# A fused recurrent-attention and SOLU kernel: two constants by transfer, the first two weight pieces fetched as one, and a weight conversion put behind the masking

## The chip, the cores and the metric

The kernel runs on one core of one Trainium2 chip. The metric is the device time of that core in microseconds: the median of the runs, lower is better.

## The reference

Four batches, eight heads, 768 tokens, head size 48; then a feed-forward block over the 3072 tokens with a hidden size of 1024. What matters of it:

```python
for t in range(S):
    state = alpha[:, :, t, :, None] * state + einsum('bhd,bhe->bhde', k[:, :, t], v[:, :, t])
    y[:, :, t] = einsum('bhd,bhde->bhe', q[:, :, t], state)
x = y.transpose(0, 2, 1, 3).reshape(B * S, H * D)       # 3072 x 384
h = x @ w_in                                            # 3072 x 1024
solu = h * softmax(h)
ln = (solu - mean(solu)) / sqrt(var(solu) + 1e-6) * g_ln
out = ln @ w_out                                        # 3072 x 384
```

q, k, v, alpha and g_ln are float32. The two weight matrices come in as 64-bit floats, since they are scaled by a 64-bit number when they are made.

## The kernel before

The 768 tokens are cut into six chunks of 128 tokens (`g`, 0 to 5), and each chunk holds all four batches. A chunk first goes through the attention part and then through the feed-forward part. All instructions are written out in one order by hand (a manual schedule), so each engine works through its own queue in the order of the code. From the second chunk on, the attention work of the next chunk is spread by a table of steps over the eight blocks of the up-projection of the present one. The first chunk has its own opening, and this opening is where the change lies.

The opening runs as follows. SyncE issues transfers of the first chunk's alpha, k, q and v (`load_first`, L153, and `load_v_first`, L189) and then of the first weights (`fetch`, L569). ScalarE's queue issues two small ones, `parity` and `g_rows`. GpSimd makes the identity matrix `ident` and the triangular `mask` out of `ones` with two selects (L652), and then fills several tiles with constants. TensorE turns alpha, k and q (`turned`, L171, a product with `ident`), and VectorE runs scans over the turned decay factors (L222) and multiplies keys and queries by them (L694, L704).

Then come the scores of the first chunk. `scores(0, 0)` makes those of heads 0 to 3, `scores(0, 1)` those of heads 4 to 7 (L281). They have to be multiplied by the triangular mask on their way out of PSUM. For heads 0 to 3, batches 2 and 3 are copied by ScalarE (L715) and multiplied by GpSimd (L716); batches 0 and 1 are done by VectorE in `masked(0, range(2))` (L292). Heads 4 to 7 of all four batches are VectorE's, in `masked(1)` (L292 too, out of the tiles a_h and a_o). `read_values(0)` (L315) multiplies the masked scores by the values, batch by batch, each batch needing all its heads; ScalarE copies the results into `x` (L351). `keys_back` (L300) and its copies `kg` (L302) and `next_state` (L364) make the state.

The 64-bit weights arrive as raw words in a tile `room` of six slots (1536 numbers each, per partition). There are eight pieces: pieces 0 to 3 are two blocks each of w_in, pieces 4 to 7 two blocks each of w_out. `fetch(i, slot, n)` transfers `n` pieces, one transfer for each of three (w_in) or two (w_out) row groups. With n = 1 a piece lies flat in its slot; with n = 2 the rows of two pieces lie beside each other over two slots, and each piece is a cut of 256 out of rows of 512 (`raws`). `bits(i)` makes 32-bit floats out of a piece with five VectorE instructions: L599 and L602 (`top`), L607 and L610 (`low`), and L611, which adds the two into the weight tile. `bits(i, 0)` is the first two of them, `bits(i, 1)` the last three. `in_range(i)` checks a piece's range with ScalarE (L586, L587).

The loop `for f in range(FC)` then runs the first chunk's eight up blocks: `up_mm` (L389) on TensorE, and `up_act`, an exponential (ScalarE, L403), a product with the block (VectorE, L404) and a square (ScalarE, L405). Pieces 2 and on are converted between them. Block 0 needs piece 0, block 2 needs piece 1. Behind block 0, `fetch(4, 3)` reuses slot 3, and the second chunk's k, q and alpha are loaded. The products of the first blocks are written into slots of `room` too.

Of the kernel before, what the change touches and what calls it, by code (L numbers as in the profile page):

```python
# [14 lines left out]
ALU = mybir.AluOpType  # L15
AX = mybir.AxisListType
P = 128
# [15 lines left out]
def fast_path(ctx, tc, q, k, v, alpha, moe_w_in, moe_w_out, moe_g_ln, out):  # L33
# [12 lines left out]
    nc = tc.nc  # L46
# [31 lines left out]
    ident = const.tile([P, P], FP, name="ident")  # L78
    mask = const.tile([P, P], FP, name="mask")
    ones = const.tile([P, P], FP, name="ones")  # L80
# [69 lines left out]
    def load_first(src, dst, g):  # L150
        t = slice(g * P, (g + 1) * P)
        for b in range(0, B, 2):
            nc.sync.dma_start(  # L153
                out=by_token(dst)[:, b : b + 2].rearrange("p b h d -> p (b h) d"),
                in_=src[b : b + 2, :, t].rearrange("b h p d -> p (b h) d"),
            )
# [27 lines left out]
    def load_v_first(slot):  # L184
        x = slots[slot].rearrange("p (n d) -> p n d", d=D)
        y = vn.rearrange("p b h d -> p (b h) d")
        xi, yi = (z.rearrange("p (n i) d -> p i n d", i=2) for z in (x, y))
        for b in range(0, B, 2):
            nc.sync.dma_start(  # L189
                out=x[:, H * b : H * b + 2 * H], in_=v[b : b + 2, :, 0:P].rearrange("b h p d -> p (b h) d")  # L190
            )
        for i in range(2):
            nc.gpsimd.tensor_copy(out=yi[:, i, :, all_of[i]], in_=xi[:, i])
# [95 lines left out]
    def masked(half, batches=range(B)):  # L289
        a = masks[half]  # L290
        for b in batches:
            nc.vector.tensor_tensor(  # L292
                out=sT[:, b, half * NP : half * NP + NP], in0=a[b], in1=mask[:, None, :].to_broadcast([P, NP, P]),
                op=ALU.mult,
            )
# [47 lines left out]
    def read_values(g, batches=range(B)):  # L343
        if 0 in batches:
            gr[g]["x"] = pair.tile([P, KC, B, P], FP, name="x")
        for b in batches:
            for n, part in enumerate(parts):
                for a, r, h, e in part:
                    y_mm(b, a, r, 0, vn[:, b, h, e], sT[:, b, h], n == len(parts) - 1)
        for b in batches:  # L350
            nc.scalar.copy(out=gr[g]["x"][:, :, b], in_=reading["y"][b])  # L351
# [200 lines left out]
    def place(i):  # L552
        kind, f = pieces[i]
        return w_out[:, f : f + 2, 0:DM] if kind else w_in[:, :, f * P : f * P + 2 * P]
# [3 lines left out]
    def fetch(i, slot, n=1):  # L558

        kind, f = pieces[i]  # L560
        w = n * F // (2 if kind else KC)
        raw = room[:, 1536 * slot : 1536 * (slot + n)].bitcast(U32).rearrange("p (c f w) -> p c f w", f=w, w=2)
        if kind:
            parts = [(slice(0, P), c, moe_w_out[(f + c) * P : (f + c + 1) * P, :]) for c in range(2)]
        else:
            parts = [(slice(0, P), c, moe_w_in[c * P : (c + 1) * P, f * P : f * P + w]) for c in range(KC)]
        for rows, c, src in parts:
            if float64:
                nc.sync.dma_start(out=raw[rows, c].rearrange("p f w -> p (f w)"), in_=src.bitcast(U32))  # L569
            else:  # L570
                dst = w_out[rows, f + c, 0:DM] if kind else w_in[rows, c, f * P : f * P + w]
                nc.sync.dma_start(out=dst, in_=src)
        for m in range(n):
            raws[i + m] = raw[:, :, w // n * m : w // n * (m + 1)]
# [14 lines left out]
    def bits(i, part=None):  # L589
        if not float64:  # L590
            return
        lo, hi = raws[i][:, :, :, 0], raws[i][:, :, :, 1]
        if part != 1:
            made[i] = [
                two.tile([P, F], FP, tag="two", name=x).rearrange("p (c f) -> p c f", c=hi.shape[1])
                for x in ("top", "low")
            ]
            top = made[i][0].bitcast(U32)
            nc.vector.tensor_scalar(  # L599
                out=top, in0=hi, scalar1=3, scalar2=0x3FFFFFF8, op0=ALU.logical_shift_left, op1=ALU.bitwise_and  # L600
            )
            nc.vector.scalar_tensor_tensor(  # L602
                out=top, in0=hi, scalar=0xC0000000, in1=top, op0=ALU.bitwise_and, op1=ALU.bitwise_or
            )
        if part != 0:
            top, low = made.pop(i)
            nc.vector.tensor_scalar(  # L607
                out=low.bitcast(U32), in0=top.bitcast(U32), scalar1=0xFF800000, scalar2=None, op0=ALU.bitwise_and
            )
            nc.vector.scalar_tensor_tensor(out=low, in0=lo, scalar=2.0**-52, in1=low, op0=ALU.mult, op1=ALU.mult)  # L610
            nc.vector.tensor_tensor(out=place(i), in0=low, in1=top, op=ALU.add)  # L611
# [34 lines left out]
    def inline(x, name):  # L646
        return nc.inline_tensor(np.ascontiguousarray(x, np.float32), name=name).ap()

    load_first(alpha, an, 0)
    nc.vector.memset(ones, 1.0)  # L650
    for x, op in ((ident, ALU.is_equal), (mask, ALU.is_ge)):
        nc.gpsimd.affine_select(  # L652
            out=x, in_=ones, pattern=[[1, P]], compare_op=op, fill=0.0, base=0, channel_multiplier=-1
        )
    odd = np.arange(P) // E1 % 2
    nc.scalar.dma_start(out=parity, in_=inline(np.stack([1 - odd, odd], 1), "parity_c"))
    nc.scalar.dma_start(out=g_rows, in_=moe_g_ln.rearrange("(c p) -> c p", p=P))
# [7 lines left out]
    nc.gpsimd.memset(seed, 0.0)  # L665
    nc.gpsimd.memset(state, 0.0)
    load_v_first(0)
    fetch(0, 3)
    fetch(1, 4)
    fetch(2, 1, 2)  # L670
    nc.vector.memset(small_ones, 1.0 / 32)
    nc.vector.memset(mhalf, -0.5)
    nc.vector.memset(mone, -1.0)
# [26 lines left out]
    for i in (2, 0, 1):  # L700
        if i == 1:
# [3 lines left out]
            out=qe if i == 2 else qv[:, part], in0=t[i], in1=aT[:, part, 1:SW], op=ALU.mult  # L705
# [9 lines left out]
        nc.scalar.copy(out=s, in_=masks[0][b])  # L715
        nc.gpsimd.tensor_tensor(out=s, in0=s, in1=mask[:, None, :].to_broadcast([P, NP, P]), op=ALU.mult)  # L716
    masked(0, range(2))
    bits(0, 0)
    masked(1)
    bits(0, 1)  # L720
    read_values(0)
    gains()
    keys_back(0)
# [225 lines left out]
    def compare(out, x, bound, op):  # L949
# [6 lines left out]
        out=chunks[:, :, 2], in0=sums[:, :, 2], scalar=0.25, in1=sums[:, :, 3], op0=ALU.mult, op1=ALU.is_le  # L956
# [6 lines left out]
    else:  # L963
# [9 lines left out]
        out=bad, in0=all_ok[0:1, 0:1], scalar1=float(P * ends[-1]), scalar2=None, op0=ALU.is_lt  # L973
# [415 lines left out]
def kernel(tc, *args):  # L1389

    with ExitStack() as ctx:
        taken = fast_path(ctx, tc, *args)
    with tc.If(taken > 0):
        general_path(tc, *args)
# [30 lines left out]
```

## Time and profile before

| | |
|---|---|
| median of 3 runs | 382.29 us (382.2 to 382.33) |
| profiled execution, its own time | 382.33 us |
| its span, from the first to the last instruction | 380.6 us |
| granted TensorE clock | 0.998 |
| TensorE busy | 366.1 us, 96% of the span |
| VectorE, ScalarE, GpSimd busy | 244.7, 146.5 and 131.0 us |
| HBM read and written | 25.17 and 4.72 MB |

The rows of the profile give start and length in microseconds, the engine (PE is TensorE, PEld its weight loads, DVE VectorE, ACT ScalarE, POOL GpSimd, SP SyncE), the line of the kernel, the operation, the tile written and the tiles read, shapes as partitions x elements, and a count where several instructions are merged. In square brackets stands how long the engine was idle before and what released it. `room<-h,sT` reads: room is written, from h and sT. Times count from the span's start.

### The profile page before, as it was taken

The page shows a single profiled execution, that of the slowest core. Times are in us where ns is not written, and L with a number is a line of the kernel's source. Part 1 is how long each engine was busy: PE and PEld are TensorE (multiplying, and loading weights), DVE is VectorE, ACT ScalarE, POOL GpSimd, SP SyncE. Part 2 cuts the span into 40 slices and gives each one's busy share as a digit, 9 for nine tenths or more (in the row PEclk, how much of TensorE's full clock was granted, in tenths as well). Part 3 has the DMA queues.
Part 4 walks back from the last instruction along what each step waited for, and adds up shares of the span by engine and source line. Part 5 has one row for each costly group of instructions (what it writes and reads, how often), then busy time and mean ns, then how long its engine had stood idle before and what let it go on. Part 6 is the DMA issues. An engine that isn't in the chain of part 4 may idle for free.

```text
span 380.6 us, 10529 instructions
## 1 busy us (share of the span) xinstructions
PE 366.1 (96%) x4659; PEld 220.3 (58%) x4659; DVE 244.7 (64%) x379; ACT 146.5 (38%) x263; POOL 131.0 (34%) x136
## 2 busy tenths in 40 slices
PE   8869999999998999999999999999999999999995
PEld 8666345557654566555576555575555675555552
DVE  0997878997998776883665874665875411455410
ACT  2627775484355253215351224351224131233110
POOL 5050000041148980663630662630672520333210
PEclk9999999999999999999999999999999999999999
DMA  9994969304089000960001950002400000000011
GB/s 178 182 307 124 213 223 189 88 0 127 24 188 161 7 7 9 199 146 22 22 14 35 208 122 22 23 24 40 67 0 22 22 24 2 22 21 21 22 46 47
DMA packets 65670, 30.65 MB, mean 81 GB/s; under 512 B 47048, under 2 KB 63440, under 8 KB 65616
## 3 DMA queue, kind: packets, MB, share of 16 engines
q1 hardware_dynamic: 64880, 29.11, 34.9%
q8 instruction: 38, 0.62, 0.7%
q10 hardware_dynamic: 736, 0.79, 0.6%
q14 instruction: 16, 0.13, 0.1%
HBM read 25.17 MB, written 4.72 MB: 79 GB/s over the span
## 4 chain that ended last, share of the span: by engine, by line
PE 72%; DVE 15%; ACT 7%; issue 3%; DMA 1%; SPq 0%; ACTq 0%; DVEq 0%
PE o L500 30%; PE h L389 24%; PE y L315 8%; PE a L281 5%; DVE hT L222 3%; DVE room L404 2%; PE warm L445 2%; DVE sT L292 2%; DVE top L602 2%; DMA an<-in_alpha_dram 1%; ACT sq L586 1%; DVE aT L197 1%; PE kv L364 1%; PE tp L300 1%; DVE top L599 1%
## 5 line engine op out<-in xcount | busy, mean ns | idle before, releaser
L500 PE MATMUL o<-w_out,room 128*128 128x385 f32 x384 | 133.8, 491 | 0.0
L389 PE MATMUL h<-x,w_in 128*128 128x512 f32 x288 | 132.3, 598 | 0.5 <-DVE room L404 0.5
L500 PEld LDWEIGHTS o<-w_out,room 128*128 128x128 f32 x384 | 71.2, 190 | 55.8 <-issue 13.7
L389 PEld LDWEIGHTS h<-x,w_in 128*128 128x128 f32 x288 | 52.8, 189 | 59.4 <-issue 48.2
L404 DVE TENSOR_TENSOR room<-h,e 128x512 f32<-128x512 f32 x40 | 27.6, 689 | 81.5 <-ACT e L403 81.4
L403 ACT ACTIVATE e<-h 128x512 f32<-128x512 f32 x40 | 23.9, 596 | 107.6 <-PE h L389 107.6
L420 POOL TENSOR_TENSOR p<-p,e 128x512 f32<-128x512 f32 x30 | 41.8, 1394 | 15.7 <-ACT e L403 15.6
L537 POOL TENSOR_TENSOR r<-sums,mhalf 128x1 f32<-128x1 f32 x20 | 14.9, 746 | 80.6 <-DVE sums L528 80.5
L405 ACT ACTIVATE u<-room 128x512 f32<-128x512 f32 x40 | 25.2, 630 | 38.5 <-DVE room L404 38.5
L292 DVE TENSOR_TENSOR sT<-a,mask 128x512 f32<-128x512 f32 x42 | 26.1, 682 | 8.3 <-PE a L281 8.2
L263 POOL TENSOR_TENSOR state<-state,hT 128x192 f32<-128x192 f32 x20 | 11.2, 580 | 53.7 <-DVE hT L222 53.7
L243 POOL TENSOR_TENSOR kT<-kT,hT 128x1024 f32<-128x1024 f32 (+1 forms) x8 | 14.2, 1798 | 42.6 <-DVE kT L197 34.3
L222 DVE TENSOR_TENSOR_SCAN hT<-aT,unit 128x516 f32<-128x516 f32 x18 | 23.2, 1364 | 8.6 <-ACT aT L686 8.5
L315 PE MATMUL y<-sT,vn 128*32 128x128 f32 x768 | 23.3, 274 | 4.0 <-DVE sT L292 2.9
L281 PEld LDWEIGHTS a<-qv,kT 32*128 32x128 f32 x704 | 21.8, 186 | 9.1 <-issue 2.4
L420 DVE TENSOR_TENSOR p<-p,u 128x512 f32<-128x512 f32 x30 | 22.7, 756 | 6.5 <-ACT u L405 6.5
L222 DVE TENSOR_TENSOR_SCAN aT<-aT,seed 128x516 f32<-128x516 f32 x18 | 26.6, 1510 | 0.2
L281 PE MATMUL a<-qv,kT 32*128 32x128 f32 x704 | 24.5, 278 | 2.3 <-DVE qv L704 0.9
L315 PEld LDWEIGHTS y<-sT,vn 128*32 128x32 f32 x768 | 20.7, 110 | 6.0 <-DVE sT L292 3.1
L214 ACT ACTIVATE sq<-an,mone 128x1536 uint8<-128x1536 f32 x12 | 18.9, 1572 | 0.2
L315 PE MATMUL y<-qv,state 32*32 32x128 f32 x960 | 16.8, 277 | 0.3 <-issue 0.3
L539 ACT ACTIVATE o_sb<-o,r 128x384 f32<-128x384 f32 x16 | 9.3, 580 | 18.8 <-POOL r L537 18.8
(148 smaller groups left out, 376.3 us busy)
## 6 DMA issues: line engine op xcount, KB each, us to landing
an<-in_alpha_dram SPq DMA_DIRECT2D x20, 192.0 KB, 4.0
vn<-in_v_dram SPq DMA_DIRECT2D x10, 384.0 KB, 6.2
out_dram<-o_sb SPq DMA_DIRECT2D x20, 192.0 KB, 1.9
room<-in_moe_w_out_dram SPq DMA_DIRECT2D x8, 384.0 KB, 3.6
kn<-in_k_dram SPq DMA_DIRECT2D x16, 192.0 KB, 4.7
qn<-in_q_dram SPq DMA_DIRECT2D x16, 192.0 KB, 3.5
kn<-in_k_dram SPq DMA_DIRECT2D x4, 384.0 KB, 5.6
qn<-in_q_dram SPq DMA_DIRECT2D x4, 384.0 KB, 5.7
```

The costliest lines, as they stand in the source:

```text
L214: nc.scalar.activation(out=sq, in_=x, func=AF.Relu, scale=sign, bias=mone, accum_out=over[:, g, i : i + 1])
L222: nc.vector.tensor_tensor_scan(out=o, data0=a, data1=s, initial=1.0, op0=ALU.mult, op1=ALU.add)
L281: nc.tensor.matmul(a[b][:, i], lhsT=kT[quarter(b), kb], rhs=qv[quarter(b), qb], start=kb == h, stop=kb != h, tile_position=(32 * b, 0), sk ...
L292: nc.vector.tensor_tensor(out=sT[:, b, half * NP : half * NP + NP], in0=a[b], in1=mask[:, None, :].to_broadcast([P, NP, P]), op=ALU.mult,)
L315: nc.tensor.matmul(y_bank(b)[quarter(r), a], lhsT=lhsT, rhs=rhs, start=(b, r) not in begun, stop=stop, tile_position=(row, 32 * r), skip_g ...
L389: nc.tensor.matmul(h, lhsT=w_in[:, a, f * P : (f + 1) * P], rhs=d["x"][:, a].rearrange("p b t -> p (b t)"), start=(a == 0), stop=(a == KC ...
L403: nc.scalar.activation(out=e, in_=h, func=AF.Exp)
L404: nc.vector.tensor_tensor(out=u, in0=h, in1=e, op=ALU.mult)
L405: nc.scalar.activation(out=u2, in_=u, func=AF.Square)
L420: eng.tensor_tensor(out=p, in0=d[0][i] if f == 1 else p, in1=d[f][i], op=ALU.add)
L500: nc.tensor.matmul(d["o"][:, 0 : DM + 1], lhsT=u_of(g, f)[:, b * P : b * P + P], rhs=w_out[:, f], start=(f == 0), stop=(f == FC - 1), skip ...
L537: nc.gpsimd.tensor_tensor(out=r, in0=s[:, 3:4], in1=mhalf, op=ALU.pow)
```

## The change

Its short description names several things at the second up-projection ("fourth chunk's finish behind the first exponential, a forward scan ahead of the first block, queries' last 16 turned one block sooner") "in place of: First weight pieces fetched apart". The steps at the second up-projection are in the code of both versions. What differs is this:

- `ident` and `mask` are no longer made by GpSimd. They are constants in memory (128x128 numbers, 64 KB each), brought in by two transfers that ScalarE's queue issues ahead of `parity` and `g_rows`. The fill of `ones` stands later in the code, but is still the first of VectorE's fills.
- Weight pieces 0 and 1 are fetched as one into slots 3 and 4 (three transfers with rows of 4 KB), where they were two fetches (six transfers with rows of 2 KB).
- `masked(1)` stands ahead of the whole of `bits(0)`, where `bits(0)` was cut in two around it.

```diff
--- before.py
+++ after.py
@@ -647,11 +647,8 @@
         return nc.inline_tensor(np.ascontiguousarray(x, np.float32), name=name).ap()
 
     load_first(alpha, an, 0)
-    nc.vector.memset(ones, 1.0)
-    for x, op in ((ident, ALU.is_equal), (mask, ALU.is_ge)):
-        nc.gpsimd.affine_select(
-            out=x, in_=ones, pattern=[[1, P]], compare_op=op, fill=0.0, base=0, channel_multiplier=-1
-        )
+    nc.scalar.dma_start(out=ident, in_=inline(np.eye(P), "ident_c"))
+    nc.scalar.dma_start(out=mask, in_=inline(np.triu(np.ones((P, P))), "mask_c"))
     odd = np.arange(P) // E1 % 2
     nc.scalar.dma_start(out=parity, in_=inline(np.stack([1 - odd, odd], 1), "parity_c"))
     nc.scalar.dma_start(out=g_rows, in_=moe_g_ln.rearrange("(c p) -> c p", p=P))
@@ -665,9 +662,9 @@
     nc.gpsimd.memset(seed, 0.0)
     nc.gpsimd.memset(state, 0.0)
     load_v_first(0)
-    fetch(0, 3)
-    fetch(1, 4)
+    fetch(0, 3, 2)
     fetch(2, 1, 2)
+    nc.vector.memset(ones, 1.0)
     nc.vector.memset(small_ones, 1.0 / 32)
     nc.vector.memset(mhalf, -0.5)
     nc.vector.memset(mone, -1.0)
@@ -715,9 +712,8 @@
         nc.scalar.copy(out=s, in_=masks[0][b])
         nc.gpsimd.tensor_tensor(out=s, in0=s, in1=mask[:, None, :].to_broadcast([P, NP, P]), op=ALU.mult)
     masked(0, range(2))
-    bits(0, 0)
     masked(1)
-    bits(0, 1)
+    bits(0)
     read_values(0)
     gains()
     keys_back(0)
```

## The prediction

> **What bounds the kernel now.** I read the page first, then the chain of work that ended last up to 70 us, then the timeline of that stretch engine by engine, and last the landings of the weight transfers.
>
> ```profile
> span 380.6 us, 10529 instructions
> ...
> PE 366.1 (96%) x4659; PEld 220.3 (58%) x4659; DVE 244.7 (64%) x379; ACT 146.5 (38%) x263; POOL 131.0 (34%) x136
> ```
>
> TensorE is full on average, so the body is a queue of its work: whatever delays the first up-projection delays all that follows. From 130 us on it is busy for all but about 5 us of 250 (the table by stretches). The diff touches only work before 35 us, where the chain runs otherwise (columns: start, length, what):
>
> ```profile
> 21.10 1.27 DVE sT L292 x2
> 22.37 1.16 DVE top L599
> 23.55 1.90 DVE top L602
> 25.45 0.61 DVE sT L292
> 26.06 0.04 issue
> 26.11 3.69 PE y L315 x124
> ```
>
> VectorE masks two quarters of the first half of the scores (L292), then does two steps of the first weight piece's conversion (L599, L602), and only then masks the second half; TensorE's reading of the values (L315) waits for that. The timeline of the same stretch:
>
> ```profile
> 21.83 2.80 POOL L716 TENSOR_TENSOR sT<-sT,mask 128x512 f32<-128x512 f32 x2 [0.47 <-ACT sT L715]
> ...
> 22.28 1.23 DVE L599 TENSOR_SCALAR top<-room 128x768 uint32<-128x768 uint32 x1
> ...
> 23.55 1.90 DVE L602 SCALAR_TENSOR_TENSOR top<-room,top 128x768 uint32<-128x768 uint32 x1
> ...
> 25.37 1.27 DVE L292 TENSOR_TENSOR sT<-a_h,mask 128x512 f32<-128x512 f32 x2
> 26.10 3.42 PEld L315 LDWEIGHTS y<-sT,vn 128*32 128x32 f32 x124 [3.14 <-DVE sT L292]
> ...
> 30.29 0.55 DVE L599 TENSOR_SCALAR top<-room 128x768 uint32<-128x768 uint32 x1
> ...
> 31.24 2.74 PE L389 MATMUL h<-x,w_in 128*128 128x512 f32 x6
> ...
> 35.97 0.58 ACT L403 ACTIVATE sT<-h 128x512 f32<-128x512 f32 x1
> ...
> 36.64 0.69 DVE L404 TENSOR_TENSOR room<-h,sT 128x512 f32<-128x512 f32 x1 [2.15 <-ACT sT L403]
> ...
> 37.24 0.96 DVE L599 TENSOR_SCALAR top<-room 128x768 uint32<-128x768 uint32 x1
> ```
>
> Two things are to be seen. TensorE stands still for some 3 us for two conversion steps that nobody needs yet. And these two take 1.23 and 1.90 us while GpSimd multiplies by the mask (21.83 to 24.63), but 0.55 and 0.96 with GpSimd idle (30.29; the next row of that piece). The last of the second half's scores ends at 22.90 (22.62 + 0.28), just after VectorE turned to the conversion.
>
> **The masking moved ahead of the conversion.** VectorE ends the first masking at 22.37 and now waits for the scores until about 22.95. Four maskings take 2.40 (25.37 to the next start, 27.77), to 25.35 instead of 27.77. GpSimd is still at work beside them, but the pair at 21.08, half beside it, took 0.68 to 0.69 each against 0.67 alone. TensorE waits only for the first masking, so L315 starts at 22.95 + 0.69 = 23.64: 2.46 sooner. GpSimd's two quarters are ready by 24.63, TensorE reaches the last quarter at 23.64 + 3 x 0.92 = 26.4.
>
> Everything queued behind on ScalarE moves by the same 2.46: the x copies, the three kg copies, two range checks (32.01 to 35.97), so the first exponential can start at 33.5.
>
> **The conversion of pieces 0 and 1.** It starts at 25.35 if the weights are there, after GpSimd's masks. Fetched as one, both pieces are now 256-wide cuts of 512-wide rows, as pieces 2 and 3 are today; those took 0.96 and 0.94 in L599 (37.24, 43.75) where the pieces fetched alone take 0.55. So I take 1.00 + 1.06 + 0.59 + 1.00 + 0.96 = 4.61 us a piece, by starts: the first from 37.24, the others from piece 1 (30.88, 31.94, 32.53, 33.53, end 34.49). Piece 0 is done at 29.96 (30.30 before), piece 1, with g_col's 0.08 between, at 34.65 (34.49 before). So VectorE loses 0.58 by waiting, 2 x 0.45 by the cut rows, wins about 1.6 by being clear of GpSimd, and ends where it was. What is won is the order.
>
> The page "VectorE: DVE Perf Modes" of the Trainium skill (section "What auto-detection actually checks") speaks against this edit: a one-source op in SBUF gets the doubled mode only with outermost dimensions both even or equal, and three cut rows against a flat destination are neither. The 0.96 and 0.94 agree with it; were it not to hold here, with 0.55 for both pieces, the gain would be about 0.3 larger. [...]
>
> **What that makes of the first blocks.** The first up matmul waits for piece 0: 29.98 against 31.24. The first product (L404) waits for VectorE: 34.65 against 36.64, which is 1.99 sooner; its 2.15 us of waiting are gone. Then TensorE takes 2.66 for the first block, 1.5 for the state (L364), 7.99 for blocks 1 to 3: free at 42.13, and block 4 began at 43.89. Block 1's product: ScalarE's square ends at 36.0, the state copies at 36.96, the exponential at 37.6, so 37.6 against 39.39. Block 2's: its square and range check end at 40.85, exponential to 41.4, against 43.14. Block 4 therefore starts 1.74 sooner; block 3's product, after the key copy, 1.7 sooner. VectorE is 97% busy from 60 to 70 and TensorE nearly full after, and I find only transfers that don't move along: the second chunk's keys landed at 40.81 and are copied at 44.41, the queries at 44.82 for 48.77, so a shift of 1.7 fits.
>
> SP's queue behind this: the fetch into slot 3 (issued 33.07) must now wait for both pieces, to about 33.6, and the keys, queries and alpha behind it go 0.5 later: keys 41.3, wanted at 42.7. That cover is 1.4.
>
> **The identity and the mask by transfer.** GpSimd loses two selects of 0.29 and starts its fills 1.1 sooner; its next wait is for v at 19.02, so nothing. ScalarE's queue issues two more transfers ahead of the table load (0.39 and 0.67 are the two rows there): 0.8 to 1.3, against waiting for alpha until 6.47 after being done at 3.4. Nothing. The identity is wanted at 7.82, the mask at 21.08; the parity table issued at 0.80 landed at 2.69. The packets are 256 of 512 bytes, 16 per DMA engine, 27 ns each for g_rows' rows of that size: 0.43 us on all that shares the engines, at most. Alpha 6.39 to 6.8: TensorE's warm-up runs to 7.89. Keys 9.99 to 10.4: wanted at 10.46. Queries: TensorE 0.4 later, its last 16 dimensions at 16.95, wanted at 17.58. Values: GpSimd's copies end at 21.8, its masks begin at 21.83. If these covers were gone it would cost 0.43 at most. The ones fill stays first on VectorE: no change.
>
> **The fetch.** Six transfers of 256 KB become three of 512 KB. In the trace's record of landings, piece 0's three landed by 21.61, piece 1's by 25.94, pieces 2 and 3 (512 KB each) by 28.46. Both pieces are now complete only with the last. The late bound is 25.94 + 0.43 = 26.4. The early one goes by the rate of the 4 KB rows: pieces 2 and 3 moved at 387 to 428 GB/s between 25 and 27 us, so 1.57 MB take 3.9 us; from the first weight packets at about 17.9 plus 0.43, with 1.3 for late engines as seen there, 23.5. I take 24.5, in time for 25.35, with a cover of 0.9; each us past 25.35 costs one us.
>
> **The sum.** The smallest shift along both paths, 1.7 us, off the profiled execution's 382.33 (span 380.6, and 1.7 around it; the median is 382.29): 380.6. A gain of 2.0 is the most (the first product's shift).
>
> **Rivals.**
> 1. The weights end last. Landed at 26.4, the conversion starts 1.05 late and the gain is 0.65: 381.7. For it: the parts of piece 1's last transfer landed over 2.8 us (23.10 to 25.94). Against: larger rows flowed faster.
> 2. Slower: the joined transfers finish among pieces 2 and 3, because the same engines serve all six. At 28.46 + 0.43 = 28.9 the conversion starts 3.5 late: first product at 38.2, 1.5 later than now, 383.8. It decides from a landing at 27.1 (no gain left). Against: each engine took the pieces in order; no piece-1 landing was later than the first engine of pieces 2 and 3 by over 1 us (25.94 against 24.96).
> 3. The shift is lost again before 100 us, to VectorE's full stretch or a transfer: about 382.2. The dense chain speaks against it.
> 4. The change isn't what its words say: block orders of the second up are in both versions and not in the diff, so they give nothing. That is sure and in the sum.
>
> **How the numbers follow.** A measurement of this kernel can tell about 0.2% (0.76 us) from no change. Forecast, 380.1 to 381.5: 0.73. Rival 1 at its late end, 381.5 to 382.2: 0.11; rival 3: 0.05; rival 2 with anything else that delays the start: 0.11. Faster 0.73, within 0.2% 0.15 (rival 1's end, rival 3), slower 0.12. The range is 380.1 (gain 2.0 and a little) to 382.2.
>
> **What would show it.** Right: the maskings of a_h and a_o directly behind those of a, L315 from 23.6, L599 at 0.96 for all of the first four pieces and L602 at 0.96 throughout, L404's first at about 34.7. Wrong: a wait of L599 for a transfer at 25.4 (rival 1 up to 27, rival 2 past it), or a first L404 at 34.7 with a fifth up block no sooner than 43.9.

## The result, and the profile after

The changed kernel took 380.5 us (median of 4 runs, 380.0 to 380.82) against 382.31 for the kernel before (4 runs, 382.2 to 382.61): a ratio of 0.995, with a 95% interval of 0.9933 to 0.9967. That is 1.8 us less. The profiled execution took 380.48 with a span of 378.7, 1.9 below the span before.

The page of the changed kernel:

```profile
span 378.7 us, 10523 instructions
...
PE 365.5 (97%) x4659; PEld 219.2 (58%) x4659; DVE 244.1 (64%) x379; ACT 146.8 (39%) x263; POOL 129.4 (34%) x134
```

The engines' work is the same to within 2 us, so the gain must be idle time. GpSimd's two selects are what it has fewer. The chain of work that ended last, in the same stretch as before:

```profile
22.10 0.68 DVE sT L292
22.82 1.07 PE y L315 x23
23.89 1.49 issue
25.38 3.04 PE y L315 x101
28.42 0.15 PE tp_g L622
```

The two conversion steps are off the chain, and the reading of the values follows the first masking of the second half at once. New is a hold of 1.49 us in the middle of it for which the trace names no cause. The rows of VectorE and ScalarE that answer to those shown of before:

```profile
22.08 1.29 DVE L292 TENSOR_TENSOR sT<-a_h,mask 128x512 f32<-128x512 f32 x2 [0.55 <-PE a_o L281]
...
25.28 0.95 DVE L599 TENSOR_SCALAR top<-room 128x768 uint32<-128x768 uint32 x1 [0.72 <-DMA room<-in_moe_w_in_dram]
26.27 0.96 DVE L602 SCALAR_TENSOR_TENSOR top<-room,top 128x768 uint32<-128x768 uint32 x1
...
29.81 0.94 DVE L599 TENSOR_SCALAR top<-room 128x768 uint32<-128x768 uint32 x1
...
35.28 0.69 DVE L404 TENSOR_TENSOR room<-h,sT 128x512 f32<-128x512 f32 x1 [0.88 <-ACT sT L403]
```

```profile
34.61 0.58 ACT L403 ACTIVATE sT<-h 128x512 f32<-128x512 f32 x1
```

The conversion now waits 0.72 us for the joined transfer, its first step takes 0.95 for both pieces, and the first product still waits for the exponential. From 45 to 95 us every engine runs 1.35 us ahead of the first profile of before; after 200 us it is 1.72, the rest having come at the readings of the values (L315) of later chunks, where TensorE was held for 0.7 us in all against 1.4 before, for "issue" both times. That difference also appears between two profiles of one and the same kernel, so I don't give it to the change.

One thing in the profile after needed an explanation before the sum could be trusted: the first masking began at 20.24, 0.84 sooner than before, although nothing ahead of it had become cheaper. The warm-up products of TensorE at the very start (columns: start, length, engine, line) took 5.38 us:

```profile
1.04 5.38 PE L445 MATMUL warm<-ones 128*128 128x128 f32 x32 [1.04 <-DVE w_out L671]
```

In the first profile of the kernel before they took 6.78:

```profile
1.11 6.78 PE L445 MATMUL warm<-ones 128*128 128x128 f32 x32 [1.11 <-DVE w_out L674]
```

### The profile page after: what moved, and what is told of

It reads as the page before. It is cut to its first block, busy times and chain, and to the rows that moved or that the text cites. A ratio compares the mean times of both kernels' runs of the same rounds, so it can differ in the third digit from the quotient of the medians.

```text
span 378.7 us, 10523 instructions
## 1 busy us (share of the span) xinstructions
PE 365.5 (97%) x4659; PEld 219.2 (58%) x4659; DVE 244.1 (64%) x379; ACT 146.8 (39%) x263; POOL 129.4 (34%) x134
## 3 DMA queue, kind: packets, MB, share of 16 engines
HBM read 25.30 MB, written 4.72 MB: 79 GB/s over the span
## 4 chain that ended last, share of the span: by engine, by line
PE 74%; DVE 11%; DMA 4%; ACT 4%; SPq 3%; issue 2%; ACTq 0%
PE o L500 30%; PE h L389 26%; PE y L315 8%; PE a L281 5%; DMA an<-in_alpha_dram 3%; SPq L153 2%; DVE hT L222 2%; DMA qn<-in_q_dram 2%; DVE sT L292 1%; PE kv L364 1%; PE tp L300 1%; DVE aT L197 1%; DVE room L404 1%; SPq L141 1%; ACT sq L214 1%
## 5 line engine op out<-in xcount | busy, mean ns | idle before, releaser
L404 DVE TENSOR_TENSOR room<-h,e 128x512 f32<-128x512 f32 x40 | 27.6, 690 | 81.2 <-ACT e L403 81.1
L281 PE MATMUL a<-qv,kT 32*128 32x128 f32 x704 | 24.5, 278 | 1.7 <-POOL qv L254 0.8
L315 PE MATMUL y<-sT,vn 128*32 128x128 f32 x768 | 23.6, 274 | 2.6 <-issue 2.1
L315 PEld LDWEIGHTS y<-sT,vn 128*32 128x32 f32 x768 | 20.9, 110 | 4.8 <-issue 3.8
L315 PE MATMUL y<-qv,state 32*32 32x128 f32 x960 | 16.7, 277 | 0.1
```

The costliest lines, as they stand in the source:

```text
L281: nc.tensor.matmul(a[b][:, i], lhsT=kT[quarter(b), kb], rhs=qv[quarter(b), qb], start=kb == h, stop=kb != h, tile_position=(32 * b, 0), sk ...
L315: nc.tensor.matmul(y_bank(b)[quarter(r), a], lhsT=lhsT, rhs=rhs, start=(b, r) not in begun, stop=stop, tile_position=(row, 32 * r), skip_g ...
L404: nc.vector.tensor_tensor(out=u, in0=h, in1=e, op=ALU.mult)
```

## The experiments

Theory A is the prediction's: the order of masking and conversion makes the gain. The others are named in the texts on record. Each kernel was measured beside the kernel before on the same chip. There are three such sets: the first four rows of the table, with before at 382.74 us (median), the next four at 382.84 and the last three at 382.54. Ratios and intervals are those on record; they can differ a little from the quotient of the two medians.

| kernel | us | ratio to before | 95% interval |
|---|---|---|---|
| before, unchanged | 382.55 | 0.9995 | 0.9978 to 1.0012 |
| masking moved alone | 379.46 | 0.9916 | 0.9892 to 0.9940 |
| constants by transfer alone | 382.85 | 1.0004 | 0.9988 to 1.0021 |
| pieces fetched as one alone | 384.68 | 1.0043 | 1.0017 to 1.0070 |
| changed kernel, unchanged | 380.84 | 0.9934 | 0.9915 to 0.9954 |
| moved, constants by transfer | 380.03 | 0.9919 | 0.9903 to 0.9936 |
| moved, pieces fetched as one | 380.42 | 0.9938 | 0.9918 to 0.9957 |
| before, TensorE kept busy | 381.78 | 0.9969 | 0.9953 to 0.9985 |
| moved, range check later | 380.07 | 0.9935 | 0.9921 to 0.9948 |
| moved, twelve warm-up products | 380.04 | 0.9936 | 0.9922 to 0.9949 |
| masking moved alone, again | 379.68 | 0.9928 | 0.9915 to 0.9942 |

**The kernel before, once more.**

> The kernel before, unchanged, for a second profile of it. Theory A (the order of masking and conversion is the whole gain): nothing to learn, 382.3 us. Theory B (the warm-up products of TensorE, 5.38 us long after the change against 6.78 before, are shorter by chance, because the point at which TensorE's products get twice as fast is at another place in each execution): the warm-up here is another length than 6.78 us, anywhere from 4.5 to 7, while the time stays within 0.3 us of 382.3. If the length is 6.78 again and 5.38 in every kernel with the constants by transfer, the change itself makes it shorter.

TensorE's timeline of this second profile of the same program:

```profile
1.11 5.34 PE L445 MATMUL warm<-ones 128*128 128x128 f32 x32 [1.11 <-DVE w_out L674]
...
24.96 5.23 PE L315 MATMUL y<-sT,vn 128*32 128x128 f32 x124 [2.87 <-DVE sT L292]
```

Theory B holds: the warm-up is as short here as after the change, and the time is 382.55. The first masking stands at 19.93, sooner than in either other profile. But the 124 products of L315 took 5.23 us, where the first profile had 3.69. The stretch from 25 to 28 us, in the first profile of before and then in the second (busy time of PE, PEld, DVE, ACT, POOL, then the granted clock, the DMA share, GB/s):

```profile
25.00:28.00 3.00, 1.89 (x70) 1.90 (x74) 3.00 (x6) 0.48 (x1) 0.00 (x0) 1.00 0.97 389
```

```profile
25.00:28.00 3.00, 3.00 (x60) 2.85 (x64) 2.97 (x5) 0.48 (x1) 0.00 (x0) 0.50 0.78 317
```

The granted clock (the share of its full speed that TensorE was given) is 0.50 in the second. The trace's record of it has full clock from 4.28 us, half from 24.76 to 28.17, and full again. So these two executions (382.33 and 382.48 us) came to the same length in two ways: full clock late (7.31 us), a late start, no halving; or full clock early (4.28), an early start, and 3.41 us of half clock at the end of the 2.87 us of standing still. The second won 1.15 us at the start of L315 (24.96 against 26.11) and lost 1.54 in its run.

The mean granted clock of an execution tells the two forms apart: it was 0.991 to 0.995 in the three profiles of this study with a halving and 0.997 to 1.000 in the ten without. By this the halving is the rule for the kernel before. Of its 66 executions in these experiments, 55 had 0.991 to 0.996 and took 382.1 to 384.17 us (median 382.79; those at 0.996, which no profile had, 382.23 or more), and 11 had 0.998 or 0.999 and took 381.46 to 382.2 (median 381.58). So a halving goes with about 1.2 us more, and that the two profiles agree in length is chance: the first, with the latest full clock of all thirteen profiles, is longer than any of these 11. Every execution with the masking moved (45) or with TensorE kept busy (9) had 0.997 or more.

The page "TensorE: Matmul & The Clock Gate" of the Trainium skill (Part 1) says that the clock is decided over windows of 3413 ns which run freely, so that the point of change shifts from one execution to the next. The halved stretch here was 3413 ns long and began 20480 ns, six such windows, behind the first change; the first change lay between 4.28 and 7.31 us in the profiles of this study.

**The masking moved alone.**

```diff
-    bits(0, 0)
     masked(1)
-    bits(0, 1)
+    bits(0)
```

> Only the masking is put ahead of the conversion; the constants stay GpSimd's and the pieces are fetched apart. Theory A: the whole gain and a little more, 380.0 to 380.6: VectorE's first step L599 waits for nothing, and takes 0.55 us. Rival C (the joined fetch or the constants carry a part of the gain): 381 or more. In the profile: L315 starts within 0.1 us of the first masking's end, and is then held for 1 to 1.5 us for nothing that the profile shows, as after the change, if the hold belongs to the order.

It gained more than the whole change and more than was expected (379.46 against 380.0 to 380.6): 0.9916, and 0.9928 the second time. Its rows of VectorE and of TensorE:

```profile
24.65 0.55 DVE L599 TENSOR_SCALAR top<-room 128x768 uint32<-128x768 uint32 x1
25.24 0.96 DVE L602 SCALAR_TENSOR_TENSOR top<-room,top 128x768 uint32<-128x768 uint32 x1
...
34.75 0.69 DVE L404 TENSOR_TENSOR room<-h,sT 128x512 f32<-128x512 f32 x1 [1.77 <-ACT sT L403]
```

```profile
22.16 0.41 PE L315 MATMUL y<-sT,vn 128*32 128x128 f32 x4
23.00 1.07 PE L315 MATMUL y<-sT,vn 128*32 128x128 f32 x23 [0.42 <-DVE sT L292]
24.84 3.04 PE L315 MATMUL y<-sT,vn 128*32 128x128 f32 x101 [0.78 <-issue]
```

The conversion waits for nothing, takes the short form, and the clock's record has no halving (1.00 from 5.93 us on). The hold behind the 27th product of L315 (4 that need no second masking, and 23) is there too, so it belongs to the order; it is 0.78 us here, shorter than the 1 to 1.5 expected.

**The constants by transfer alone.** The fill of `ones` stands later here too, as in the changed kernel.

```diff
-    for x, op in ((ident, ALU.is_equal), (mask, ALU.is_ge)):
-        nc.gpsimd.affine_select(...)
+    nc.scalar.dma_start(out=ident, in_=inline(np.eye(P), "ident_c"))
+    nc.scalar.dma_start(out=mask, in_=inline(np.triu(np.ones((P, P))), "mask_c"))
```

> Only the two constants come by transfer. Theory A: no change within 0.2 us, 382.2 to 382.6. Rival C (taking two selects from GpSimd and the earlier start pay): 381.3 to 381.6, the 0.84 us by which the first masking stood sooner after the change. Rival D (the 128 KB more on the shared engines delay the queries): 382.7 to 383.

No change. The queries landed at 14.54 instead of 14.32 to 14.37; the half clock was there (25.30 to 28.71):

```profile
25.13 5.35 PE L315 MATMUL y<-sT,vn 128*32 128x128 f32 x124 [2.87 <-DVE sT L292]
```

The first masking stood at 20.10, but at 19.93 in the second profile of before, which has no constants by transfer. The 0.84 us of the first masking is therefore not theirs.

**The pieces fetched as one alone.**

```diff
-    fetch(0, 3)
-    fetch(1, 4)
+    fetch(0, 3, 2)
```

> Only the two pieces are fetched as one; the conversion's first two steps still stand ahead of the second masking. My account of the trace: the conversion at 22.3 us now waits for both pieces, which landed at 25.16 after the change, so the second masking starts at 27.2 (L599 0.96, L602 0.96) instead of 25.37: slower by 1.5 to 2, 384 us. Rival C (larger rows land so much sooner that it pays by itself): 382.3 or less.

As expected, 1.9 us slower by the medians: VectorE stands still for the transfer, with the second masking queued behind it, and TensorE for longer still. Its rows of VectorE and TensorE, and the stretch of 28 to 32 us with the granted clock of 0.50:

```profile
24.77 0.95 DVE L599 TENSOR_SCALAR top<-room 128x768 uint32<-128x768 uint32 x1 [3.13 <-DMA room<-in_moe_w_in_dram]
```

```profile
27.37 6.46 PE L315 MATMUL y<-sT,vn 128*32 128x128 f32 x124 [4.86 <-DVE sT L292]
```

```profile
28.00:32.00 4.00, 4.00 (x84) 3.77 (x78) 3.50 (x5) 0.96 (x2) 0.00 (x0) 0.50 0.02 4
```

Here the half clock lasted 6.83 us, from 26.26 on. My account had left the clock out, and most of the cost goes with it: nine of the twelve executions, with a mean clock of 0.991 to 0.996, took 383.2 to 386.2 us, and the three at 0.998 or 0.999 took 381.58 to 382.14, at most some tenths more than before at such a clock (381.46 to 381.69, six executions of this set).

**The changed kernel and its two halves beside each other.** The second kernel is the changed one with `fetch(0, 3)` and `fetch(1, 4)` again, the third the changed one with GpSimd's selects again.

> The changed kernel, unchanged, beside the next three. In the first runs the joined fetch alone cost 0.43% and the masking moved alone gained 0.84%. Theory A2 (the move gains about 3 us, the joined fetch gives back about 1.4): 0.995 of before again, with L599 waiting 0.5 to 1 us for the transfer. Rival E (the chip of the first measurement was another one and the parts don't add): the same 0.991 as the move alone.

> The changed kernel with the two pieces fetched apart: the masking moved and the constants by transfer. Theory A2: 0.9916 of before, as the move alone, so 1 to 1.5 us faster than the changed kernel; L599 0.55 and without a wait. Rival D (the constants' 128 KB cost on the shared engines): 0.994 or more.

> The changed kernel with identity and mask made by GpSimd again: the masking moved and the pieces joined. Theory A2: the changed kernel's time, 0.995 of before. Rival C (the constants carry a gain of the changed kernel): 0.997 or more.

Rival C of the third falls (0.9938, where 0.997 or more was its sign), and so does rival D: with the pieces apart and the constants by transfer it was 0.9919, as the move alone. Rival E is not decided: the changed kernel's 0.9934 lies between its 0.991 and the 0.995 of theory A2, and its interval (0.9915 to 0.9954) holds the move alone's 0.9916 and 0.995. Theory A2's size was off: the joined fetch costs 0.8 us by the medians (380.84 against 380.03), less than the 1 to 1.5 expected. The intervals overlap, and in the profiles the cost isn't in the opening: the first product stood at 34.82 in the changed kernel and at 35.16 with the pieces apart, because the hold was 0.71 in one and 1.29 in the other and ScalarE, not the conversion, came last in both. The wait for the transfer was 0.72, 0.34 and none in the three profiles of the joined fetch with the move. So: a cost of some tenths, its size open.

**The kernel before with TensorE kept busy.**

```diff
     masked(0, range(2))
+    warm(11, ps_a, "a3")
     bits(0, 0)
```

> The kernel before, with eleven idle products of ones in TensorE's queue between the scores and the reading of the values (their result is used by nothing), so that TensorE doesn't stand still there. Theory F (a part of the move's gain is TensorE's rate: after 2.9 us of standing still the 124 products of L315 took 5.23 us in the second profile of before, and 3.69 in the first): L315 takes 3.7 us here whatever the execution, and the time is 0.5 to 1.5 us below before and scatters less. Theory A (only the order counts): the time of before within 0.3 us.

```profile
21.82 2.72 PE L445 MATMUL warm<-ones 128*128 128x128 f32 x22
24.47 0.41 PE L315 MATMUL y<-sT,vn 128*32 128x128 f32 x4
25.44 3.69 PE L315 MATMUL y<-sT,vn 128*32 128x128 f32 x124 [0.56 <-DVE sT L292]
```

Idle work made the kernel faster: 0.9969, about 1.2 us (0.6 to 1.8 by the interval), with L315 at 3.69, no halving in the clock's record, and runs from 380.86 to 382.47. Theory F holds. What is left of the move's 2.9 to 3.3 us, about 1.7 to 2.1, is the order itself. Executions of the same clock agree: at 0.998 or more, before took 381.54 us in the first set (median of six) and 381.86 in the third (of three), against 379.46 and 379.68 for the masking moved alone, which is 2.1 and 2.2.

**Where the hold comes from, and the next wait.**

```diff
-    warm(16)
+    warm(12)
```

> The masking moved, and twelve warm-up products instead of sixteen. Theory I (the hold of L315 behind its 27th product is TensorE's code coming in, since a 16 KB packet of the instruction queue ends 1.3 to 1.5 us before it goes on in every kernel with the move): with 16 instructions fewer ahead of it, which are 8 pairs of a load and a product, the hold stands behind the 35th product. Rival J (the hold is a wait for data, of the second batch's masks or a PSUM bank): it stays at the 27th. Time: that of the move alone within 0.4 us, since the queries' landing at 14.4 bounds the start.

```profile
22.45 1.10 PE L315 MATMUL y<-sT,vn 128*32 128x128 f32 x31 [0.42 <-DVE sT L292]
24.85 2.82 PE L315 MATMUL y<-sT,vn 128*32 128x128 f32 x93 [1.30 <-issue]
```

With the 4 products that need no second masking, 31 make the 35th: the hold moved by eight products when sixteen instructions ahead of it were gone. It stands at a place in the code and not at a datum: rival J falls, and the place is the one that theory I gives. That the 16 KB packets of the instruction queue are what it waits for is argued from their times and not shown by itself: in each of the eight profiles with the move one ends 1.3 to 1.5 us before L315 goes on. In the first profile of before one ended at 24.41, 1.7 us before L315 began, and L315 ran through.

```diff
     bits(1)
-    in_range(1)
     ...
             next_state(0)
+            in_range(1)
             fetch(4, 3)
```

> The masking moved, the constants GpSimd's, the pieces apart, and the range check of piece 1 put behind block 0's exponential, square and state products instead of ahead of them (ScalarE waits for nothing there: VectorE waited 1.77 to 2.26 us for the first exponential in the kernels with the move). Theory G (with the move, ScalarE's two range checks of 2.03 us are the next wait): the first product at 33 instead of 34.8, 0.5 to 1.5 us below the move alone. Rival H (what is won there is lost at block 1 or 2, where ScalarE is as full): the same as the move alone within 0.4 us.

> The masking moved alone, once more, beside the two others: 0.9916 of before as in the first runs, with the hold behind the 27th product of L315 and no halved clock.

VectorE's products of blocks 0 and 1 (L404), first with the range check later, then with the move alone:

```profile
32.90 0.68 DVE L404 TENSOR_TENSOR room<-h,sT 128x512 f32<-128x512 f32 x1
...
37.48 0.69 DVE L404 TENSOR_TENSOR room<-h,sT 128x512 f32<-128x512 f32 x1 [2.05 <-ACT sT L403]
```

```profile
34.37 0.69 DVE L404 TENSOR_TENSOR room<-h,sT 128x512 f32<-128x512 f32 x1 [1.17 <-ACT sT L403]
...
37.13 0.69 DVE L404 TENSOR_TENSOR room<-h,sT 128x512 f32<-128x512 f32 x1 [0.19 <-ACT sT L403]
```

Rival H: 1.47 us won at block 0 are gone at block 1, where the same check stands ahead of the second exponential. The masking moved alone has the lowest medians of this study (379.46 and 379.68); the two variants beside its second row (380.07 and 380.04) can't be told from it by their intervals.

## Why the prediction was right or wrong

The time (380.6 predicted, 380.5 measured) and the main reason were right: the masking moved alone gains at least as much as the whole change. But three terms were not what I had put. Two of them, the run of L315 and the clock of the kernel before, nearly cancelled, and the third, the cover of the joined fetch, did not come last on the way to the first product. That the number came out so close is partly luck.

- **The move: right to 0.01 us.** L315 starts 2.58 us behind the first masking's start (20.24 to 22.82), against 5.03 in both profiles of before: 2.45 less, predicted 2.46. VectorE's wait for the scores was 0.55 (0.58 predicted); L602 fell from 1.90 to 0.96 away from GpSimd.
- **L315's run: wrong.** I let it run at 3.7 us from there. It took 5.60 (22.82 to 28.42), since it was held at a place in the code (argued above: the code had not come in); before, it was not held there. So the x copies and the first exponential came at 25.84 and 34.61, not at 24.8 and 33.5, and the first product at 35.28, not 34.65, although the first masking stood 0.84 sooner than in my sum. I had VectorE's conversion come last at the first product; it was ScalarE's exponential, and the wait for it did not vanish, it fell from 2.15 to 0.88.
- **The kernel before was read from one execution.** I took its clock as full from 7.31 us on, as that trace shows it. Against this trace the sum is: the move -2.45, the first masking 0.84 sooner, L315 longer by 1.91, together -1.38, which is the 1.35 by which the engines are ahead from 45 us on. In the second profile, and by the clock in 55 of 66 executions, it halves at the gap that the move closes, and the sum against that one is: the move -2.45, a first masking later by 0.31, L315 longer by 0.37 (5.60 against 5.23), together -1.77, which is the 1.73 by which the engines are ahead at 60 us. The gain of not halving (1.54) and the loss by the hold (1.91) are nearly equal, and this is why 1.7 came out.
- **The cover of the joined fetch: mis-sized.** I had it land at 24.5 with 0.9 to spare. It landed at 25.16, at rival 1's side of my range though not at its end, and with the first masking sooner the wait was 0.72. The row price was right: 0.95 and 0.94 for L599, as pieces 2 and 3 had shown. The sum of the conversion has a small slip, "2 x 0.45 by the cut rows": its own rows give 2 x 0.41 (1.00 against 0.59). That the joined fetch alone makes the kernel slower shows how much of it the move hides.
- **The constants: right**, nothing measurable. Their cost on the queries was 0.2 to 0.3 us (bound: 0.43).
- **Rivals 2 and 3** did not come true. The joined transfers landed ahead of pieces 2 and 3, and the shift held to the end. Rival 4 was no doubt but a certainty, and it was in the sum.

## What to carry to other kernels

In an in-order queue, ask who waits for the instruction behind the one that fills a gap: filling 0.6 us of VectorE's idle time held TensorE back by 2.5, and the conversion was no sooner for it. A sum that is made from one trace contains that execution's clock; where an engine stands still for about 3 us, take a second profile of the same program before you believe the term. And when an engine starts sooner, look at what else had been arriving in its idle time; here, as far as is argued, that was code.

## What the runs showed of the hardware that I had not expected

- TensorE's granted clock went to 0.50 for 3.41 us around the end of 2.87 us of standing still (second profile of before, constants alone), and for 6.83 us from within 4.86 (joined fetch alone). In the first profile of before, with the same 2.87, it stayed at 1.00. Eleven products of ones in the gap were worth 1.2 us.
- TensorE was held at one place in the code for 0.2 to 1.5 us in seven of the eight profiles with the move; in the eighth (range check later) the product there came 0.39 us after the one ahead of it. The place moved by exactly eight products when sixteen instructions ahead of it went away.
- Two profiles of one program (the move alone) differ by 0.59 us at 200 us, mostly by such holds (0.78 against 0.20 at the first).
